# Moving an evacuation copy ahead of the gates, exchanging two banks of the last down projection, and beginning sums earlier, in a fused attention and feed-forward kernel

## The chip, the cores and the metric

The kernel runs on one core of a Trainium2 chip. The metric is the device time of one execution in microseconds (us). The profiler also gives, for each run, the span of the core (here 1.8 us below the device time) and the mean granted TensorE clock.

Names: PE is TensorE, PEld its weight loads, ACT is ScalarE, DVE is VectorE, POOL is GpSimd, SP the engine whose queue issues most transfers. A bank is one of the eight pieces of PSUM, 512 float32 values in each of 128 partitions, in which this kernel's matmuls leave their results; it has to be emptied by ACT or DVE before TensorE writes it again.

## The reference, cut to what matters

```python
xn = layernorm(x)                                    # x: 2048 x 448
s  = attention(xn @ wq, last 512 keys and values) @ wo   # 16 heads of 256, 8 key/value heads
g  = silu((gelu(xn @ w_gate) * (xn @ w_up)) @ w_down)    # hidden size 1792
return x + s * g
```

## The kernel before

A list of operations is written in program order; every engine then runs its own part in that order, with a semaphore wait wherever it reads or overwrites what another engine made. So the order in the source is the order in each engine's queue.

The 2048 rows are four chunks of 512. The feed-forward part comes first. Its down projection (`@ w_down`) of chunks 1, 2 and 3 is done with seven half-size products in place of eight (a Strassen scheme): DVE forms sums of activation blocks (`sum_act`) and weight blocks (`sum_wd`), TensorE makes seven products of 14 matmuls each in six banks, and DVE and ACT combine them and apply the silu ("the gates"). Chunks 2 and 3 are interleaved with the first attention heads.

```python
# sums ahead of chunk 1's down projection: (earliest step, function, arguments); a step is two groups
DN_SUMS = [(26, sum_act, (1, k, 0)) for k in range(4)] + [(28, sum_act, (1, k, 1)) for k in range(4)] + [
    (28, sum_wd, x) for x in ((4, 4, 0), (5, 2, 4), (6, 5, 0), (3, 1, 5))]
...
def down7(c, banks, g, b_g, order=(3, 6, 5, 4, 2, 1), then=None):
    B1, B4, B6, B7, B5, B3 = banks
    ...
    def sums(q, b, V, bV):                     # x: sum, y: its tanh
        x, bx = Cs[q % 2]                      # two buffers "cd"
        if V is None:
            act(x[:, :], bank[b][:, 0:D], ACT.Copy, (b_ps[b],), (bx,), scale=F)
        else:
            plus(x[:, :], [bx], b, V, bV)      # DVE: bank * F + V
        y, by = Ts[q % len(Ts)]                # buffers "th"
        act(y[:, :], x[:, :], ACT.Tanh, (bx,), (by,), scale=0.5)
    ...                                        # gate, store, what: product -> its bank and operand
    product(0, B1, A(0, 0))
    act(U2, bank[B1][:, 0:D], ACT.Copy, (b_ps[B1],), bU2, scale=F)
    for j in order:
        product(j, *what[j], j != 1)           # product 1 is added onto B1, last
    if then:
        then()
    plus(U2, bU2, B6, U2, bU2)
    plus(U3, bU3, B7, U2, bU2)
    sums(0, B4, U3, bU3)
    sums(1, B5, U3, bU3)
    gate(0, 1, 0)                              # DVE: (th + 1) * cd
    plus(U2, bU2, B5, U2, bU2)
    sums(2, B3, U2, bU2)
    gate(1, 1, 1)
    store(1)
    sums(3, B1, None, None)                    # the copy out of B1, then its tanh
    gate(2, 0, 1)
    ...                                        # gate(3, 0, 0), store(0)
...
for m in range(NS):                            # heads; AB: banks of the scores, BB: of the values
    if m in groups:
        for i in range(m, hi, 2):
            q_group(i, ...)                    # queries; ACT and DVE copy them out of the banks
            if m == 0:
                for k in range(2):
                    sum_act(2, 2 * p + k)
    ...
    s_mm(m)                                    # scores, exp (ACT), normalise (DVE), transpose (SP)
    if m < LAG:                                # LAG = 2
        if m == 0:
            down7(2, (BB[0], BB[1], AB[2], AB[3], BB[2], BB[3]), g2w, b_g2w,
                  then=lambda: [sum_act(3, k) for k in range(4)])()
            ...
        else:
            down7(3, (BB[0], BB[1], AB[2], AB[3], BB[2], BB[3]), g2w, b_g2w, (3, 4, 2, 5, 6, 1))()
        if m == LAG - 1:
            ...                                # loads of gate and x tiles on the POOL queue
    if len(late) == LAG:
        pv(late.pop(0))                        # values of the head two back: BB[0], BB[1] first
    late.append(m)
```

The softmax here doesn't subtract the row's maximum and nothing guards it: scores larger than these inputs give would overflow.

## Time and profile before

| | before |
|---|---|
| device time, first three runs | 549.36, 551.25, 551.12 us |
| span of the profiled run | 549.4 us, mean granted clock 0.997 |
| TensorE busy | 536.3 us (98%) |
| TensorE's waits from 74 to 160 us | 6.1 us in four (a fifth in the list, 0.2 us for `qT`, stands where a matmul record is missing) |
| half-clock stretch | 136.46 to 139.83 us |

In a timeline each row is a run of like instructions: start, length, engine, source line, what it writes and reads, and in brackets the idle time before it with what ended it. Lengths overlap, since matmuls are pipelined; to see what a row costs, subtract its start from the next row's. Some records are missing: a row of "x7" that should have eight began one matmul (0.216 us) earlier.

### The profile page before, as it was taken

How to read it: one execution, taken by the hardware profiler on the slowest of the kernel's cores; microseconds unless marked ns; L12 is line 12 of the kernel's file. 1: busy time of each engine (PE TensorE's matmuls, PEld its weight loads, DVE VectorE, ACT ScalarE, POOL GpSimd, SP SyncE). 2: the span in 40 equal slices, each digit the busy share in tenths (PEclk: the TensorE clock that was granted, in tenths of full speed). 3: DMA queues.
4: the chain of work that ended last, by engine and by line, in shares of the span. 5: the costliest groups of instructions: out<-in, count | busy, mean ns of one | idle time of the engine just before them, and what ended most of it. 6: DMA issues, size and time to landing. Idle time of an engine off the chain costs nothing.

```text
span 549.4 us, 10770 instructions
## 1 busy us (share of the span) xinstructions
PE 536.3 (98%) x4081; PEld 306.8 (56%) x4106; DVE 376.4 (69%) x823; ACT 314.0 (57%) x784; POOL 39.3 (7%) x78
## 2 busy tenths in 40 slices
PE   9999999997899999999999999999999999999997
PEld 5554447456744444794444459644444884444487
DVE  6673885798566757863775777467667934776775
ACT  5433664873367858404884870278578206876820
POOL 1130400000020000001101000020000003001010
PEclk9999999999999999999999999999999999999999
DMA  9569262912299766501672570056447502773631
GB/s 291 123 192 126 58 117 56 297 47 56 57 176 198 148 150 116 116 1 43 149 154 65 135 154 20 1 135 153 101 85 163 81 1 68 153 163 76 152 56 33
DMA packets 171459, 61.36 MB, mean 112 GB/s; under 512 B 154960, under 2 KB 168272, under 8 KB 171408
## 3 DMA queue, kind: packets, MB, share of 16 engines
q1 hardware_dynamic: 167632, 51.39, 43.7%
q0 software_dynamic: 3008, 8.72, 7.0%
q8 instruction: 32, 0.52, 0.4%
q10 hardware_dynamic: 768, 0.57, 0.3%
q14 instruction: 19, 0.16, 0.1%
HBM read 19.76 MB, written 3.67 MB: 43 GB/s over the span
## 4 chain that ended last, share of the span: by engine, by line
PE 87%; DVE 8%; ACT 3%; issue 2%; ACTq 0%; DVEq 0%
PE bank L390 86%; ACT p L837 2%; DVE actTh L557 1%; DVE pn L844 1%; DVE wt L384 1%; PE bank L507 1%; DVE actTh L384 1%; DVE sd L384 1%; DVE tmp L608 1%; DVE cd L608 0%; DVE wdt L384 0%; DVE qT L822 0%; ACT th L381 0%; DVE rden L841 0%; ACT gl L381 0%
## 5 line engine op out<-in xcount | busy, mean ns | idle before, releaser
L837 ACT ACTIVATE p<-bank 128x512 f32<-128x512 f32 x256 | 150.4, 596 | 26.0 <-DVE pn L844 23.8
L390 PE MATMUL bank<-pT,va 128*128 128x512 bf16 x512 | 120.8, 379 | 2.0 <-ACT cd L381 2.0
L390 PE MATMUL bank<-kT,qT 128*128 128x512 bf16 x487 | 118.0, 379 | 2.4 <-ACT qT L381 1.1
L844 DVE TENSOR_SCALAR pn<-p,rden 128x512 bf16<-128x512 f32 x256 | 113.1, 484 | 8.6 <-DMA pT<-pn 4.4
L390 PE MATMUL bank<-xnT,wq 64*128 64x512 bf16 x768 | 94.9, 376 | 0.0
L390 PEld LDWEIGHTS bank<-pT,va 128*128 128x128 bf16 x512 | 49.9, 98 | 62.6 <-ACT cd L381 2.5
L390 PE MATMUL bank<-xnT,wgu 64*128 64x512 bf16 (+2 forms) x768 | 84.0, 350 | 0.1
L390 PEld LDWEIGHTS bank<-kT,qT 128*128 128x128 bf16 x512 | 49.2, 98 | 62.0 <-issue 3.8
L381 ACT ACTIVATE qT<-bank 128x512 bf16<-128x512 f32 x76 | 44.1, 596 | 54.3 <-PE bank L390 52.7
L822 DVE CAST qT<-bank 128x512 bf16<-128x512 f32 x52 | 34.9, 690 | 51.6 <-PE bank L390 51.6
L390 PEld LDWEIGHTS bank<-xnT,wq 64*128 64x128 bf16 x768 | 36.7, 94 | 46.4 <-ACT p L837 2.0
L390 PEld LDWEIGHTS bank<-xnT,wgu 64*128 64x128 bf16 x768 | 37.1, 94 | 36.8 <-issue 0.6
L841 DVE RECIPROCAL rden<-rsum 128x2 f32<-128x2 f32 x128 | 21.2, 165 | 48.1 <-ACT p L837 48.1
L837 ACT ACTIVATION_READ_ACCUMULATOR p<-bank 128x1 f32 x256 | 51.6, 202 | 0.0
L381 ACT ACTIVATE gl<-bank 128x512 bf16<-128x512 f32 x56 | 33.2, 597 | 29.3 <-PE bank L390 26.4
L390 PE MATMUL bank<-wt,sr 128*128 128x224 f16 x512 | 49.7, 259 | 0.0
L390 PEld LDWEIGHTS bank<-wt,sr 128*128 128x128 f16 x512 | 49.1, 98 | 0.0
L381 ACT ACTIVATE xnT<-bank 128x224 bf16<-128x224 f32 (+2 forms) x12 | 4.4, 400 | 71.9 <-PE bank L390 70.9
L862 DVE TENSOR_SCALAR oTh<-bank 128x512 f16<-128x512 f32 x62 | 42.3, 683 | 0.0
L381 ACT ACTIVATE oTh<-bank 128x512 f16<-128x512 f32 x66 | 38.9, 589 | 4.6 <-PE bank L390 4.6
L390 PE MATMUL bank<-wt,oTh 128*128 128x224 f16 x384 | 38.3, 259 | 0.3 <-ACT oTh L381 0.3
L390 PEld LDWEIGHTS bank<-wt,oTh 128*128 128x128 f16 x384 | 36.7, 98 | 1.8 <-ACT oTh L381 1.1
(77 smaller groups left out, 409.9 us busy)
## 6 DMA issues: line engine op xcount, KB each, us to landing
wtb<-in_A_wo_dram POOLq DMA_DIRECT2D x4, 896.0 KB, 10.5
wq<-in_A_wq_dram SPq DMA_DIRECT2D x2, 1536.0 KB, 7.5
va<-in_A_v_cache_dram SPq DMA_DIRECT2D x8, 256.0 KB, 3.5
pT<-pn SPq DMA_TRANSPOSE x128, 2.8
xr<-in_A_x_dram POOLq DMA_DIRECT2D x15, 112.0 KB, 2.3
wd<-in_B_w_down_dram SPq DMA_DIRECT2D x1, 1568.0 KB, 8.5
g<-g_all POOLq DMA_DIRECT2D x14, 112.0 KB, 2.3
out_dram<-xr POOLq DMA_DIRECT2D x12, 112.0 KB, 2.2
```

Of the source, the lines that this page charges most:

```text
L381: K.op("act", lambda e, o=o, i=i: e.activation(o, i, func, scale=scale), reads, writes)
L384: K.op(eng, lambda e: e.tensor_tensor(o, x, y, op), reads, writes)
L390: ins = e.matmul(o, lhsT=l, rhs=r, start=st, stop=sp, skip_group_check=True)
L507: ins = e.matmul(bank[b][:, 0:w], lhsT=gl[:, 0, 0:P], rhs=gl[:, 0, 0:w], start=True, stop=True)
L557: K.op("dve", lambda e: e.tensor_tensor(o[:, c % 2, f, :], bank[b + 1], gl[:, s, :], ALU.mult), (b_ps[b + 1], b_gl[s]), (b_actT[c % 2][f],))
L608: K.op("dve", lambda e: e.scalar_tensor_tensor(out=o, in0=bank[b][:, 0:D], scalar=F, in1=V, op0=ALU.mult, op1=ALU.add), [b_ps[b]] + bV, bo)
L822: K.op("dve", lambda v, s=s, b=b: v.tensor_copy(qT[:, s, 1, :], bank[b + 1]), (b_ps[b + 1],), (b_qT[s][1],))
L837: K.op("act", lambda e, b=b, r=r, z=z: e.activation(p32[:, z, :], bank[b], ACT.Exp, scale=att_scale, accum_out=rsum[:, r:r + 1]), (b_ps[b] ...
L841: K.op("dve", lambda e, r=r: e.reciprocal(rden[:, r - 1:r + 1], rsum[:, r - 1:r + 1]), b_rsum[r - 1:r + 1], b_rden[r - 1:r + 1])
L844: K.op("dve", lambda e, r=r - 1 + t, z=(n - 1 + t) % NP32, y=y, t=t: e.tensor_scalar(pn[:, y, t, :], p32[:, z, :], rden[:, r:r + 1], None, ...
L862: K.op("dve", lambda v, i=i, b=b: v.tensor_scalar(oTh[:, i, :], bank[b], WS, None, op0=ALU.mult), (b_ps[b],), (b_oT[i],))
```

## The change

The intent: (1) put the weight sums of chunk 1 earlier, so that TensorE does not wait for the last one; (2) begin chunk 2's sums ahead of the query copies; (3) let ACT empty bank B1 into a third buffer ahead of the last two gates; (4) in chunk 3 exchange B1 and B4, so that its first product takes the bank that is emptied first. Cut to its core (the placing of the buffers is left out):

```diff
-        DN_SUMS = [(26, sum_act, (1, k, 0)) ...] + [(28, sum_act, (1, k, 1)) ...] + [(28, sum_wd, x) ...]
+        DN_SUMS = [(24, sum_act, (1, k, 0)) ...] + [(30, sum_wd, x) ...] + [(34, sum_act, (1, k, 1)) ...]
-            for i in range(1):                               # casts of the weights, per step
+            for i in range(2 if n >= 24 else 1):
-            for i in range(2 if n in (28, 30, 32, 34, 36) else 1):
+            for i in range(2 if n in (30, 32, 34, 36) else 1):
@@ down7
-                x, bx = Cs[q % 2]
-                if V is None:
-                    act(x[:, :], bank[b][:, 0:D], ACT.Copy, (b_ps[b],), (bx,), scale=F)
-                else:
+                x, bx = Cs[(0, 1, 0, 2)[q]]
+                if b is not None:
                     plus(x[:, :], [bx], b, V, bV)
...
             plus(U2, bU2, B5, U2, bU2)
+            act(Cs[2][0][:, :], bank[B1][:, 0:D], ACT.Copy, (b_ps[B1],), (Cs[2][1],), scale=F)
             sums(2, B3, U2, bU2)
...
-            sums(3, B1, None, None)
+            sums(3, None, None, None)
@@ heads
+        for k in range(2):
+            sum_act(2, k)                                    # ahead of the first query group
-                        for k in range(2):
-                            sum_act(2, 2 * p + k)
+                        sum_act(2, 2 + p)
...
-                    down7(3, (BB[0], BB[1], AB[2], AB[3], BB[2], BB[3]), g2w, b_g2w, (3, 4, 2, 5, 6, 1))()
+                    down7(3, (BB[1], BB[0], AB[2], AB[3], BB[2], BB[3]), g2w, b_g2w, (3, 4, 2, 5, 6, 1))()
```

## The prediction

> **What bounds the kernel now.** I began with the busy shares, which say who can set the end:
>
> ```profile
> PE 536.3 (98%) x4081; PEld 306.8 (56%) x4106; DVE 376.4 (69%) x823; ACT 314.0 (57%) x784; POOL 39.3 (7%) x78
> ```
>
> TensorE is busy for all but 13 us of the 549.4 us span, and the chain that ended last is TensorE for 87%. The change adds or removes no matmul, so it can win only TensorE's idle time and time at a reduced clock. So the second view is the list of waits, for TensorE alone between 74 and 160 us:
>
> ```profile
> PE bank L390 <- ACT cd L381: 4.4, 2, 2.4
> PE bank L390 <- DVE wdt L384: 1.1, 1, 1.1
> PE bank L390 <- ACT p L837: 0.6, 1, 0.6
> ```
>
> Four waits, 6.1 us together; all lie around the three down projections in seven products (chunks 1, 2, 3), which the change touches. Third, TensorE's timeline there (columns: start, us, instruction, in brackets the idle time before it and its releaser):
>
> ```profile
> 79.01 1.51 PE L390 MATMUL bank<-wdh,actTh 128*128 128x224 f16 x14
> 81.58 2.86 PE L390 MATMUL bank<-wdt,actTh 128*128 128x224 f16 x28 [1.05 <-DVE wdt L384]
> ...
> 123.14 1.50 PE L390 MATMUL bank<-wdt,actTh 128*128 128x224 f16 x14
> 125.19 1.51 PE L390 MATMUL bank<-wdt,actTh 128*128 128x224 f16 x14 [0.55 <-ACT p L837]
> ...
> 132.13 1.67 PE L390 MATMUL bank<-kT,qT 128*128 128x512 bf16 x7
> 136.16 2.58 PE L390 MATMUL bank<-wdh,actTh 128*128 128x224 f16 x14 [2.36 <-ACT cd L381]
> 138.53 2.15 PE L390 MATMUL bank<-wdt,actTh 128*128 128x224 f16 x14
> ...
> 147.44 1.67 PE L390 MATMUL bank<-kT,qT 128*128 128x512 bf16 x7
> 151.12 1.90 PE L390 MATMUL bank<-pT,va 128*128 128x512 bf16 x8 [2.00 <-ACT cd L381]
> 152.86 2.18 PE L390 MATMUL bank<-kT,qT 128*128 128x512 bf16 x8
> 154.87 1.89 PE L390 MATMUL bank<-pT,va 128*128 128x512 bf16 x8
> ```
>
> A product of 14 matmuls takes 1.345 us from start to start when nothing holds it, a score block of 8 takes 1.73 us (where x7 stands, one record is missing and the block began 0.2 us earlier). But the two products after the idle 2.36 us take 2.37 and 1.99 us. The fourth view, busy time and granted clock by stretch, says why (the ninth number, ahead of the DMA share, is the clock):
>
> ```profile
> 133.80:136.16 2.36, 0.00 (x1) 0.00 (x1) 2.16 (x5) 1.10 (x3) 0.00 (x0) 1.00 0.00 0
> 136.46:139.83 3.37, 3.37 (x20) 2.65 (x19) 2.13 (x6) 3.11 (x10) 0.00 (x0) 0.50 0.39 133
> ```
>
> The clock is halved for 3.37 us: 1.7 us lost beyond the wait. Last, ACT's timeline at both waits:
>
> ```profile
> 132.51 1.11 ACT L381 ACTIVATE th<-cd 128x448 f32<-128x448 f32 x2 [6.94 <-DVE cd L608]
> 135.03 0.58 ACT L381 ACTIVATE th<-cd 128x448 f32<-128x448 f32 x1 [1.41 <-DVE cd L608]
> 135.56 0.54 ACT L381 ACTIVATE cd<-bank 128x448 f32<-128x448 f32 x1
> ...
> 151.09 0.58 ACT L381 ACTIVATE th<-cd 128x448 f32<-128x448 f32 x1
> 151.58 0.59 ACT L837 ACTIVATE p<-bank 128x512 f32<-128x512 f32 x1
> ...
> 153.68 0.60 ACT L837 ACTIVATE p<-bank 128x512 f32<-128x512 f32 x1 [0.28 <-DVE pn L844]
> ```
>
> The copy that empties the first product's bank is ACT's fourth job in the gating, although its bank was complete at 132.1 and ACT idled 1.41 us just before. That bank is the one that TensorE wants next, both times.
>
> **What the Trainium skill says.** "TensorE: Matmul & The Clock Gate", section "Part 1: The HAM clock gate": the clock is either full or half, decided by activity in a free-running window of about 3.4 us; it falls after an idle window. The trace agrees on half clock and on the length (0.50 for 3.37 us), but here 2.36 us of idleness was enough. Counted back from 136.46, a window of that length would hold that wait nearly whole; the idle 2.00 us before 151.12 would straddle two, and there the clock stayed at 1.00. "Perfetto Trace Analysis", section "Matmuls": independent groups should rotate through PSUM banks so that one's evacuation overlaps the next's matmuls; the wait for `cd` is a case where they did not. "PSUM — Partial Sum Buffer", section "Engine vs sequencer instructions": ScalarE and VectorE queues are strict FIFO; so moving the copy up two places matters, and what stands behind the gating still waits.
>
> **Part by part.** (1) *Order of the weight and activation sums before chunk 1.* The second product should follow at 79.01+1.345 = 80.36, and starts at 81.58, because the weight sum `wdt` comes last on DVE. After the change the weight sums are done two pair-steps earlier (a step is 3.02 us), and what ends last is a 0.55 us activation sum that only the sixth product reads, some 5 us later. The casts, now two per step, make ACT 1.24+0.94+0.76 = 2.94 us per step, just under 3.02. **Gain 1.2 us.**
>
> (2) *Two of chunk 2's sums before the query copies.* DVE runs without a pause from the last `wt` sum at 117.2 to its first reciprocal at 123.74; it is the same four sums of 1.0 to 1.1 us and four copies of 0.6 us in another order, so the reciprocal, the fourth exp behind it, and the product at 125.19 do not move. The first query copy ends near 120.0, just when the scores want it. **Gain 0** (0.7 us if I misjudge DVE).
>
> (3) *Chunk 2 into chunk 3.* With the copy moved ahead it runs at 133.6 to 134.2, in ACT's idle time. With B1 and B4 exchanged, chunk 3's first product writes the bank that the first gating sum emptied at 132.5, and starts when the scores end, at 131.92+1.73 = 133.65 in place of 136.16: **2.5 us**. Its second product, at 135.0, writes the copied bank, free since 134.2. Banks for products 5 and 6 come free with the third and fourth exp at about 137.9 and 138.7, wanted at 139.0 and 140.4. With no gap the clock does not drop: seven products took 147.22-136.16 = 11.06 instead of 9.41: **1.65 us**.
>
> (4) *Chunk 3 into the first attention products.* Here the 2.2 us (151.12 against 148.95) will not come back whole. The value product starts at once, but the next score block needs banks emptied by four exps, which stand on ACT behind the gating. Gating is bound by DVE's chain; only the copy's 0.55 us leaves ACT's line in front of the exps, so the first exp goes from 151.58 to 151.03 (in the old frame) and the fourth ends at 153.7 in place of 154.28. The fourth score pair follows it, then the next value product at 154.3 in place of 154.87: **gain 0.56 us**. The wait for `cd` turns into some 1.5 to 1.8 us of waits for `p`.
>
> Sum: 1.2+0+2.5+1.65+0.56 = 5.9 us. Behind 155 us nothing but names changes, and TensorE is bound there, so all of it shifts. 551.12-5.9 = **545.2 us**. The timed runs support the clock's part: 549.36, 551.12, 551.25 differ by about the 1.7 us of one half-clock window, so I guess the fast one escaped it.
>
> **Rivals.** *A: both `cd` waits vanish whole.* The list of waits suggests it: 1.2+2.5+1.65+2.2 = 7.5, so 543.6 us; 8.2 with the wait in (2). Against it stands ACT's FIFO order in (4), which the change leaves, except for the copy. *B: the new waits for `p` halve the clock.* They leave TensorE about half idle over 3.5 us, between the window that dropped (about a quarter busy) and those that did not (two thirds busy). It would cost up to 1.7 us: 546.9. *C: a new wait takes the place of the old.* Query copies now stand behind two sums on DVE, and the third buffer of chunk 3 lies where a normalised tile is still being transposed; but its transpose ends about 2.5 us before the copy. A slip of 1 us in each would make 547. *D: a busier DVE or ACT in the feed-forward steps holds up matmuls.* They have two pairs of banks and DVE had 0.5 us of slack per step there; I give it little.
>
> **Range and chances.** A and part of (2) set the low end, B or C the high end: 543.8 to 547.4. Two per cent is 11 us, nearly twice all that these waits and the slow clock hold, so faster by over 2% is 0.01; slower by 2% would need a new serial chain of 11 us, 0.01.
>
> **What would show it.** Right: no TensorE wait for `wdt` near 80 us and none for `cd`; clock 1.00 throughout; chunk 3's seven products in about 9.4 us following the scores without idle; the 0.5 us wait for `p` still before chunk 2's third product; new waits for `p` before the second score block after chunk 3; ACT's copy third, not fourth, in the gating. Wrong: a `p` wait that is gone in (4), a half-clock window anywhere past the start, a wait for `qT` over 0.3 us, or a feed-forward step over 3.02 us.

## The result, and the profile after

| | before | after |
|---|---|---|
| device time, four runs each | 549.36 to 551.25, median 550.36 us | 544.97 to 546.17, median 545.96 us |
| span of the profiled run | 549.4 us | 544.4 us |
| mean granted clock of the profiled run | 0.997 | 1.000 |

The ratio is 0.9917 (95% interval 0.9892 to 0.9942), so the change gives 0.8%, under the 2% from which a run is called faster. A ratio here is the mean time of one kernel's runs over that of the other's of the same rounds, so it is not quite the ratio of the medians quoted.

TensorE's waits between 74 and 160 us in the changed kernel (total us, times, longest):

```profile
PE bank L390 <- ACT p L836: 1.7, 3, 0.9
PE bank L390 <- DVE oTh L861: 0.5, 1, 0.5
```

The waits for `wdt` and `cd` are gone. What is left is mostly `p`, the exp of the attention, and one wait that the kernel before had not: `oTh`. TensorE's timeline of the changed kernel at the same places:

```profile
79.21 1.51 PE L390 MATMUL bank<-wdh,actTh 128*128 128x224 f16 x14
80.56 2.85 PE L390 MATMUL bank<-wdt,actTh 128*128 128x224 f16 x28
...
124.17 1.51 PE L390 MATMUL bank<-wdt,actTh 128*128 128x224 f16 x14 [0.53 <-ACT p L836]
...
130.89 1.89 PE L390 MATMUL bank<-kT,qT 128*128 128x512 bf16 x8
132.62 1.50 PE L390 MATMUL bank<-wdh,actTh 128*128 128x224 f16 x14
...
142.01 1.89 PE L390 MATMUL bank<-kT,qT 128*128 128x512 bf16 x8
143.74 1.89 PE L390 MATMUL bank<-pT,va 128*128 128x512 bf16 x8
146.51 1.76 PE L390 MATMUL bank<-kT,qT 128*128 128x512 bf16 x6 [0.89 <-ACT p L836]
148.53 0.61 PE L390 MATMUL bank<-kT,qT 128*128 128x512 bf16 x2 [0.26 <-ACT p L836]
148.97 1.89 PE L390 MATMUL bank<-pT,va 128*128 128x512 bf16 x8
...
155.37 0.82 PE L390 MATMUL bank<-xnT,wq 64*128 64x512 bf16 x6 [0.51 <-DVE oTh L861]
```

The last row's counterpart in the kernel before (TensorE's timeline again) started without a wait:

```profile
160.59 0.81 PE L390 MATMUL bank<-xnT,wq 64*128 64x512 bf16 x6
```

Subtracting starts, row by row, gives the account:

| event | before | after | lead of after | gained in this stretch |
|---|---|---|---|---|
| chunk 1, first product | 79.01 | 79.21 | -0.20 | (noise of the start) |
| chunk 1, second product | 81.58 | 80.56 | 1.02 | 1.22 |
| chunk 2, third product | 125.19 | 124.17 | 1.02 | 0 |
| chunk 3, first product | 136.16 | 132.62 | 3.54 | 2.52 |
| score block after chunk 3 | 147.22 | 142.01 | 5.21 | 1.67 |
| second value product | 154.87 | 148.97 | 5.90 | 0.69 |
| second half of the second query group (of four) | 160.59 | 155.37 | 5.22 | -0.68 |
| end of the span | 549.4 | 544.4 | 5.0 | -0.2 |

(147.22 is the row at 147.44 less the missing matmul. The query group is counted from the rows: a group has 28 matmuls, and 36 precede this row.) The granted clock over chunk 3 (busy time by stretch in the changed kernel; the clock is ahead of the DMA share):

```profile
134.00:142.00 8.00, 8.00 (x86) 8.00 (x84) 5.42 (x12) 3.96 (x11) 0.00 (x0) 1.00 0.47 125
```

It is 1.00, and TensorE has no idle time in it. ACT's timeline of the changed kernel:

```profile
132.51 0.53 ACT L381 ACTIVATE cd<-bank 128x448 f32<-128x448 f32 x1
...
145.79 0.58 ACT L836 ACTIVATE p<-bank 128x512 f32<-128x512 f32 x1
...
147.79 0.60 ACT L836 ACTIVATE p<-bank 128x512 f32<-128x512 f32 x1 [0.18 <-DVE pn L843]
```

The copy now stands third, at 132.51, where the kernel before had it at 135.56. But the exps that empty the score banks still start only at 145.79, behind the gates, 2.05 us after the first value product began; so the wait that was ahead of the value product is now behind it. And DVE's timeline shows where the 0.68 us went (first the kernel before, then the changed one):

```profile
158.83 0.88 DVE L844 TENSOR_SCALAR pn<-p,rden 128x512 bf16<-128x512 f32 x2 [1.18 <-DMA pT<-pn]
```

```profile
153.83 0.88 DVE L843 TENSOR_SCALAR pn<-p,rden 128x512 bf16<-128x512 f32 x2 [2.07 <-DMA pT<-pn]
```

A normalisation waits 2.07 us (1.18 before) for a transpose of an earlier tile out of the same buffer; `oTh` and the query copies stand behind it in DVE's queue.

### The profile page after: what moved, and what is told of

It reads as the page before. It is cut to its first block, busy times and chain, and to the rows that moved or that the text cites. A ratio compares the mean times of both kernels' runs of the same rounds, so it can differ in the third digit from the quotient of the medians.

```text
span 544.4 us, 10795 instructions
## 1 busy us (share of the span) xinstructions
PE 537.4 (99%) x4106; PEld 305.8 (56%) x4106; DVE 376.1 (69%) x823; ACT 313.9 (58%) x784; POOL 39.5 (7%) x78
## 4 chain that ended last, share of the span: by engine, by line
PE 90%; DVE 5%; ACT 2%; issue 1%; DMA 1%; DVEq 0%; ACTq 0%
PE bank L390 89%; ACT p L836 2%; DVE wt L384 1%; DVE pn L843 1%; DMA pT<-pn 1%; DVE actTh L557 1%; PE bank L507 1%; DVE qT L821 0%; DVE sd L384 0%; DVE rden L840 0%; DVE cd L608 0%; DVE tmp L608 0%; ACT th L381 0%; DVE actTh L384 0%; PE bank L488 0%
## 5 line engine op out<-in xcount | busy, mean ns | idle before, releaser
L390 PE MATMUL bank<-kT,qT 128*128 128x512 bf16 x512 | 121.6, 380 | 1.1 <-ACT p L836 1.1
```

The source lines that it names most:

```text
L390: ins = e.matmul(o, lhsT=l, rhs=r, start=st, stop=sp, skip_group_check=True)
```

## The experiments

Twelve kernels ran, in three calls on three chips, with eleven runs of the kernel before in each call. These 33 runs of one kernel fall into levels that go with each run's mean granted clock:

| clock of the run | runs | span |
|---|---|---|
| 0.999 to 1.000 | 16 | 547.6 to 548.4 us |
| 0.996 to 0.997 | 15 | 549.1 to 550.4 us |
| 0.993 | 2 | 550.8 to 551.4 us |

One window of 3.41 us at half clock takes 1.7 us and lowers the mean by 3.41/2/549 = 0.003; so the levels are runs with none, one and two such windows (the runs have no trace of their own; the traces kept show one window where the mean clock is 0.997 and none where it is 0.999 or more, apart from up to 1.2 us at its very end). Medians of the kernel before thus hang on luck. Below, besides the ratio, I give the difference of mean spans to the before-runs **without a window** (547.9, 548.1 and 548.15 us); the changed kernel stands at -4.0 by this measure.

### The order of the sums alone

The kernel before with the three hunks of `DN_SUMS` and the casts alone (the first six lines of the diff above).

> The kernel before with only the new order of the sums and casts ahead of chunk 1. Theory: the wait for wdt near 80 us goes, 1.2 us less than a run of the kernel before at the same clock; the wait for cd of 2.4 us stays, and with it, in some runs, one half-clock window of 3.4 us worth 1.7 us. So about 550.0 in runs with that window and 548.2 in those without. Rival (busier ACT in the feed-forward steps): under 0.5 us gained, a step over 3.02 us.

Measured: median 550.07 us (549.72 to 551.32), ratio 0.9997 (0.9978 to 1.0016). At first sight nothing. But all six runs had a window (clock 0.997 five times, 0.994 once). Against the before-runs with one window (mean span 549.5 us) the five runs with one (548.2) are 1.4 us shorter. In the trace the second product follows without a wait, and the half clock follows the wait for `cd` (TensorE's timeline, then busy time by stretch):

```profile
80.18 2.85 PE L390 MATMUL bank<-wdt,actTh 128*128 128x224 f16 x28
...
134.77 2.24 PE L390 MATMUL bank<-wdh,actTh 128*128 128x224 f16 x14 [2.37 <-ACT cd L381]
```

```profile
135.39:138.80 3.41, 3.41 (x21) 2.69 (x19) 2.45 (x7) 2.79 (x9) 0.00 (x0) 0.50 0.30 101
```

So the gain was there, hidden by the clock. Why none of these six runs escaped, when half of the runs of before did, is not settled here; it may be chance.

### Filling the waits

Matmuls of no use, into the bank of B4, which is free by then; first in the wait ahead of chunk 3 only, then in both waits for `cd`, then both together with the new order of the sums.

```diff
+                    mms([(bank[BB[1]], ident[:, :], xnT[:, 0, 0:QC], True, True) for i in range(10)], ...)
                     down7(3, (BB[0], BB[1], AB[2], AB[3], BB[2], BB[3]), ...)()
```

and, for both, nine of the same ahead of the first `pv`.

> The kernel before with ten matmuls of 128x512 without use (into the bank of B4, which is free by then) in the wait ahead of chunk 3. The results are unchanged. Theory (the clock drops because TensorE was idle 2.4 us of one window): the wait's end does not move, the clock is 1.00 in every run, and all runs fall at 549.4 us or a few tenths above, with the 551 us runs gone. Rival (the two levels of the kernel before have another cause): the runs still lie at both 549.4 and 551.2, or all at 551.

Measured: median 551.05 us (549.59 to 551.42), ratio 1.001 (0.9988 to 1.0031). The expectation was wrong for the times: four of six runs still had one window (0.997). The profiled run had none, though the wait's end did not move; TensorE's only long wait for `cd` is now the second, and chunk 3 takes 9.4 us at full clock (the stretch shown also holds the missing matmul of the score block behind it; waits, then busy time by stretch):

```profile
PE bank L390 <- ACT cd L381: 2.2, 2, 2.0
```

```profile
135.99:145.61 9.62, 9.56 (x98) 9.50 (x100) 4.76 (x12) 3.41 (x10) 0.00 (x0) 1.00 0.39 104
```

That left the second wait, of 2.0 us, as the suspect. It is not a sure trigger: by the clock records of this trace, whose edges lie 3.413 us apart from 4.01 us on, one window ran from 147.37 to 150.79 us and held 1.92 us of that wait, and the clock stayed at 1.00. A window with 2.07 us of idle time, at the end of the kernel with the late last sum (below), was followed by half clock (busy time by stretch, this run and then that one):

```profile
147.37:150.79 3.42, 1.50 (x7) 0.70 (x8) 2.51 (x5) 2.60 (x6) 0.00 (x0) 1.00 0.21 70
```

```profile
538.77:542.18 3.41, 1.34 (x14) 1.08 (x12) 1.15 (x5) 0.56 (x2) 0.00 (x0) 1.00 0.23 64
542.18:543.30 1.12, 0.00 (x0) 0.00 (x0) 0.00 (x0) 0.00 (x0) 0.00 (x0) 0.50 0.04 9
```

So a wait of 2.0 us lies between what did and what did not drop the clock, and no trace kept shows it doing so. The two kernels that fill both waits:

> The kernel before with matmuls without use in both waits for cd: ten ahead of chunk 3 as in the run with one filling, and nine ahead of the first value product after it. Theory (either wait can drop the clock, by where the window's edge falls, so the kernel before has levels of none, one and two half-clock windows at about 549.4, 551.1 and 552.7): all runs at the lowest level, 549.2 to 549.7 us, none above 550.5. Rival (the levels have another cause): the spread of 549.4 to 552 stays.

> The same two fillings, and the new order of the sums and casts ahead of chunk 1. Theory (that order is worth 1.2 us and the timed runs of it alone hid this behind a half-clock window): 548.1 us in nearly all runs, 1.2 below the kernel with the two fillings alone. Rival (the new order costs elsewhere what it saves): the same as with the fillings alone.

Measured: with both filled 550.61 us (549.83 to 551.18), ratio 0.999 (0.9971 to 1.001); clock 0.999 or 1.000 in six of six, while seven of the eleven before-runs beside them had windows. So the clock part holds: with neither wait idle the clock never dropped. That the first wait drops it is in two traces; that the second alone can is inferred from the four runs above, which had only that one left. The expected times were wrong: the runs did not fall to the lowest level, their mean span is 0.6 us above it (548.0 to 549.4), and the spread is over 1 us at full clock. Part of it can be placed: in the traces with one and with two fillings a value product at 369 us waits 0.56 and 0.20 us for a transpose, and in the trace of the kernel before it does not. Why, 220 us behind the fillings, stays open, and so does the rest. With the new order of the sums added: 548.80 us (548.29 to 549.73), ratio 0.996 (0.9939 to 0.9982). That is 1.7 us less mean span than the fillings alone, where 1.2 was expected: the order of the sums is worth its 1.2 us or a little more, now at equal clock.

### The exchange of banks without the copy, and the copy without the exchange

```diff
-                    down7(3, (BB[0], BB[1], AB[2], ...     # kernel before
+                    down7(3, (BB[1], BB[0], AB[2], ...
```

> The kernel before with only B1 and B4 of chunk 3 exchanged. Theory: the first product follows the scores at once, the second waits some 1.15 us for the copy of the old B1, so idle time of 2.5 us becomes 1.15 and the clock no longer drops; behind chunk 3 nothing is gained, since the exps still end at the same place. 548.1 us in nearly all runs. Rival: without the earlier copy the wait only moves one product on, 551 us; or the exchange is what carries the gain, 546.5 us.

Measured: 548.15 us (548.02 to 548.47), ratio 0.996 (0.9942 to 0.9978), clock 0.999 or 1.000 in all six; -1.5 us against the runs without a window. As expected to 0.1 us. TensorE's timeline:

```profile
136.36 1.51 PE L390 MATMUL bank<-wdt,actTh 128*128 128x224 f16 x14 [1.03 <-ACT cd L381]
...
148.32 1.04 PE L390 MATMUL bank<-pT,va 128*128 128x512 bf16 x4 [1.14 <-ACT cd L381]
```

Two waits of 1.0 and 1.1 us do not drop the clock. The second wait has halved too, yet there is no gain behind chunk 3: it is the exps that set the end there.

The reverse edit in the changed kernel (copy hoisted, banks as before):

> The changed kernel without the exchange of B1 and B4. Theory: the copy ends about 0.5 us after the scores do, so chunk 3's first product waits 0.5 us and all else is as in the changed kernel: 546.4 us, clock 1.00. Rival, that the exchange carries the gain: a wait of over 1.5 us comes back and the time is 548 us or more.

Measured: 546.03 us (545.59 to 546.41), ratio 0.9921 (0.9903 to 0.9939), clock 1.000; -3.6 us, so beside the copy the exchange is worth some 0.4 us. That is a difference inside the spread of the runs; the firmer sign is the wait ahead of chunk 3, 0.3 us in this trace and none in the changed kernel's. The gains of copy and exchange overlap: the exchange alone gave 1.5 us above.

### Where chunk 2's sums stand

The changed kernel again, as the yardstick; and the changed kernel with the sums back between the query copies (the two hunks of `sum_act(2, ...)` undone).

> The changed kernel again, for comparison with the others of this call: 545.0 to 546.2 us, clock 1.00, with waits for p of about 1.2 us in the second score block after chunk 3 and 0.5 to 0.9 us before the query products that follow.

> The changed kernel with chunk 2's sums back in their old places between the query copies. Theory: the sums' places gain nothing, since DVE does the same work without a pause up to its first reciprocal; same time as the changed kernel within 0.2 us, with the 0.5 us wait for p before chunk 2's third product in both. Rival: 0.5 to 0.7 us slower.

Measured: 545.89 us (545.21 to 546.18), ratio 0.9912 (0.9896 to 0.9928), for the changed kernel; 546.10 (545.49 to 546.62), 0.9917 (0.9902 to 0.9932), with the sums back. The difference of 0.2 us is inside the spread of either. The wait is the same in both (TensorE's timeline with the sums back):

```profile
123.93 1.51 PE L390 MATMUL bank<-wdt,actTh 128*128 128x224 f16 x14 [0.56 <-ACT p L836]
```

What would have helped is to shorten DVE's line ahead of the reciprocal. The last of the four sums, needed only by the sixth product, is put behind the first head's normalisations:

```diff
-                        sum_act(2, 2 + p)
+                        if p == 0:
+                            sum_act(2, 2)
...
                 if m == 0:
+                    sum_act(2, 3)
                     down7(2, ...
```

> The changed kernel with the last of chunk 2's four sums moved behind the first head's normalisation. Theory: the reciprocal, the fourth exp and chunk 2's third product come 1.0 us earlier, the 0.5 us wait (0.7 us from start to start) goes: 0.7 us faster than the changed kernel, unless DVE's chain behind it takes it back. Rival: DVE's chain to the gating bounds this stretch, and the same wait appears ahead of chunk 3: no gain.

Measured: 545.26 us (544.68 to 545.46), ratio 0.9901 (0.9885 to 0.9917); -4.7 us against -4.0, the expected 0.7. Chunk 2's second and third products run on as one row (TensorE's timeline):

```profile
122.25 2.85 PE L390 MATMUL bank<-wdt,actTh 128*128 128x224 f16 x28
```

### The transposes and the loads beside them

The changed kernel with the five loads moved from the second head to the seventh in the source:

> The changed kernel with the five loads of x and gate tiles, which are needed only some 70 us later, issued five heads later. Theory: these loads share the transfer engines with the four transposes that follow chunk 3 and slow them (5.5 us for the first); without them the first transpose lands in about 3 us, the normalisation does not wait 2 us, and the 0.5 us wait before the query products goes: 0.8 us faster. Rival: the transposes are slow by themselves, or the queue issues them late: same time.

Measured: 545.67 us (545.29 to 546.27), ratio 0.991 (0.9896 to 0.9925). This says nothing about the theory: POOL has nothing else in its queue, so the loads were issued at 147.6 us all the same (147.7 in the changed kernel). Place in the source did not delay a transfer whose queue was empty; a dependency did, to 173.9 us in the next run. In that run the loads were made to wait for an operation of the seventh head:

```diff
+            if m == 6:
+                held = (next(o for o in reversed(K.ops) if o.eng == "act"),)
+                ...                        # the five loads, with after=held
```

> The changed kernel with the five loads of x and gate tiles made to wait for a late exp of the seventh head, so that they really leave the stretch behind chunk 3 (in the earlier try they were only moved in the queue and were issued at the same time). Theory: the first transpose lands sooner, DVE's wait for it falls from 1.3 to 2.1 us to under 1, the wait ahead of the query products goes: 0.3 to 0.8 us faster than the changed kernel, about 545.3. Rival (the transposes are slow for another reason): the wait and the time stay.

Measured: 546.67 us (546.37 to 546.84), ratio 0.9918 (0.9898 to 0.9939); -3.3 us, so 0.7 **slower** than the changed kernel, where 0.3 to 0.8 faster was expected. It was run on another chip. The mechanism was right and the sum wrong. Time from issue to landing of the transposes around chunk 3 (minimum, median, maximum), in the changed kernel and then with the loads held:

```profile
DMA to landing us min/median/max: 2.7/4.0/5.6
```

```profile
DMA to landing us min/median/max: 2.7/2.8/4.3
```

DVE waits for no transpose there any more, and the wait for `oTh` is gone. But the loads now fall among the transposes of the attention, where TensorE uses each one soon after (TensorE's timeline with the loads held):

```profile
179.77 1.90 PE L390 MATMUL bank<-pT,va 128*128 128x512 bf16 x8 [1.06 <-DMA pT<-pn]
```

The Trainium skill, "DMA: Bandwidth & Descriptors", section "Issuing engines are not separate DMA queues", says that transfers of all engines run on the same 16 DMA engines and interleave; the landing times agree: in the stretch from 125 to 165 us their median is 3.7 to 4.8 us in seven traces with the loads, and 2.8 us in both without them (the other is the last run below).

### All together

The held loads, the late last sum, and two exps of the next head ahead of ACT's last two tanh:

```diff
             act(Cs[2][0][:, :], bank[B1][:, 0:D], ACT.Copy, ...)
+            if mid:
+                mid()                      # scores and exps of two tiles of the next head
             sums(2, B3, U2, bU2)
```

> The changed kernel with three additions: the loads held back; the last of chunk 2's sums behind the first normalisation; and the first two exps of the next head put on ACT ahead of the last two gate activations, into its 1 us of idleness. Theory: no wait for p before chunk 2's third product (0.65 us), the waits for p in the second score block after chunk 3 fall from 1.2 to under 0.4 us (0.5 us gained), no wait before the query products (0.5): 544.2 us. Rival (DVE's gating chain and the transposes bound the stretch anyway): 545 us.

Measured: 545.13 us (545.03 to 545.49), ratio 0.9893 (0.987 to 0.9915); -4.7 us, the same as with the late sum alone, and what the rival said. In TensorE's timeline the wait of 0.89 us ahead of the score block is gone, but the fourth score pair still waits for its exp, which waits for DVE, and the held loads take 1.2 us back later:

```profile
147.01 0.60 PE L390 MATMUL bank<-kT,qT 128*128 128x512 bf16 x2 [0.92 <-ACT p L858]
...
178.38 1.90 PE L390 MATMUL bank<-pT,va 128*128 128x512 bf16 x8 [1.19 <-DMA pT<-pn]
```

The late sum alone is thus the version to keep: it is as fast as all three and simpler. The early exps do seem to gain: from chunk 2's second product to the second value product it is 25.65 us here (121.81 to 147.46) and 26.14 us with the late sum alone (122.25 to 148.39), so the 0.5 us that was expected. They were not run without the held loads, which would be the next experiment.

## Why the prediction was right

- **The sums of chunk 1**, 1.2 us: 1.22 in the trace; 1.4 (one window each) and 1.7 (no window) in the timed runs. Right, and visible only where the clock is the same.
- **Chunk 2's sums ahead of the queries**, 0: 0 in the trace, and undoing it changed nothing beyond the spread. Right for the stated reason: moving one sum across the reciprocal gave the 0.7 us that changing the order ahead of it could not.
- **Chunk 2 into chunk 3**, 2.5 us: 2.52. It was the copy that gave most of it; the exchange of banks, worth 1.5 us by itself, adds some 0.4 us beside the copy.
- **The clock**, 1.65 us: 1.67 in this pair of traces. But it is no fixed gain: without a window in the run of before there is none, and with two there are two. The changed kernel kept 0.999 or above in all ten of its runs. The prediction guessed this from three times; the 33 runs with their clocks bear it out. It put the full clock behind the second wait down to where the window's edge fell, and this fits: counted on from 136.43 us by 3.413 us, two windows shared that wait, with 1.0 us of idle time each. That it fell so was chance of that run; with the first wait filled, windows still came, and filling the second too removed them.
- **Chunk 3 into the first values**, 0.56 in place of the 2.2 us that the list of waits offers: 0.69. Rival A, that both waits vanish whole, is out; the exps behind the gates take over, with 1.15 us of waits for `p` in the list and 1.8 us from start to start (148.97 less 142.01 and three blocks of 1.73). Rival B, that these waits halve the clock, did not happen: they left TensorE idle for a third of 3.4 us and not for half of it. Rival D did not show either: a feed-forward step still takes 3.02 us (75.71 to 78.73 in ACT's queue).
- **The term that was missed** is -0.68 us: DVE's longer wait for a transpose, in the second query group. It is the step of the prediction that failed. The prediction had named a tile still being transposed as a risk, but for the wrong buffer and with enough time to spare; it held that behind 155 us nothing changes. In the trace with the loads held the wait is gone, so the loads that share the DMA engines are a cause of it. It varies: DVE waited 2.1 and 2.2 us in two traces of the changed kernel, and 1.4 and 1.3 us, with no wait of TensorE for `oTh`, in those with the sums back and with the banks not exchanged. Why it was longer than the 1.18 us of the kernel before, which has the same loads, is not shown.

The predicted gain was 5.9 us; the two traces give 5.9 by the second value product (6.1 in the terms above, less 0.2 at the start) and 5.0 at the end. Of the missing 0.9, 0.7 is that wait; the last 0.2 is lost at 464.6 us, where a score block takes 1.92 us in place of 1.73 with no wait in the list, and its cause stays open.

Between the medians the gain is only 4.4 us. The prediction took its 5.9 from 551.12 us, a run with a window; two of the four runs of the kernel before had times of the level without one, so on average only half of the 1.65 us was there to gain, and 0.7 us went to the missed wait. The predicted time itself, 545.2 us, does not depend on this; it is 0.8 us under the measured 545.96. One size in the prediction is also off: the waits and the slow clock hold 7.8 us (6.1 and 1.7), so the 11 us of two per cent is 1.4 times that and not nearly twice.

## What to carry to other kernels

Ask of every wait that a change removes what stands next in the same queue: here three waits were removed, and most of one of them (1.8 us from start to start) came back as a wait for the exps that had stood behind the same gates. An idle stretch of TensorE can cost more than its length: here the clock halved behind 2.4 us of it in some runs, for 1.7 us more; compare runs by their granted clock before calling a change worthless or good. And reordering work ahead of a dependency gains nothing while the engine is busy throughout; moving work across it does.

## What the Trainium skill lacked or had wrong

- "TensorE: Matmul & The Clock Gate", sections "Part 1: The HAM clock gate" and "HAM oscillation — how this bites in real kernels": it states the rule as no idle gaps of TensorE above about 3.4 us. Here single gaps of 2.36 and 2.37 us were enough, in two traces, to halve the clock for one window of 3.41 us, and 17 of 33 runs of the kernel before had a lowered clock; a window with 2.07 us of idle time was followed by half clock too, one with 1.92 us was not, and two gaps of 1.0 and 1.1 us, 12 us apart, never did it in six runs.
- The same page says that the window is free-running and the penalty varies by run. It does not say that this makes levels in the timed runs: 547.6 to 548.4, 549.1 to 550.4 and 550.8 to 551.4 us here, told apart only by the granted clock.
- "DMA: Bandwidth & Descriptors", section "Rules for kernel authors", says that a transpose next to ordinary transfers needs nothing. That is meant of correctness; it costs time. The median time of the transposes to landing was 4.0 us beside five loads of 112 KB and 2.8 us without them.
- No page says why TensorE work of no use in an idle stretch (nineteen matmuls of 128x512) made the runs 0.6 us longer at full clock; nor do these runs, beyond a wait for a transpose of 0.2 us at 369 us.
